# Attention and two expert layers on one core: the order of all five queues worked out by the kernel and fixed by order-only dependences

## The chip, the cores and the metric

One core of one Trainium2 chip runs the whole program. The metric is device time in microseconds (us); lower is better. The five queues are those of TensorE (PE; its weight loads, PEld, are issued by the same queue), VectorE (DVE), ScalarE (ACT), GpSimd (POOL) and SyncE (SP). SP only issues DMAs. Each queue works through its instructions in the order of the program that it was given; an instruction whose inputs are not there holds up all behind it on that queue.

## The reference, cut to what matters

```python
def reference(...):
    # q, k, v: batch 4, heads 8, sequence 1152, width 64
    q_pool = q.reshape(B, H, S // 2, 2, D).mean(axis=3)          # pairs of queries are averaged
    scores = scale * np.matmul(q_pool, k.transpose(0, 1, 3, 2))
    scores = scores - np.max(scores, axis=-1, keepdims=True)
    attn = np.exp(scores)
    attn = attn / (np.sum(attn, axis=-1, keepdims=True) + 1e-09)
    x = np.matmul(attn, v)                                       # then 2304 tokens x 512
    h = x @ w_in                                                 # 512 -> 2048
    x1 = np.maximum(0.01 * h, h) @ w_out                         # 2048 -> 512
    h = np.maximum(np.maximum(x1 @ w1, x1 @ w2), x1 @ w3)        # 512 -> 768, three times
    return h @ w2_out                                            # 768 -> 512
```

The weights of the expert layers come as 64-bit floats.

## The kernel before, in words

The work is cut by batch (4) and, within attention, by pairs of heads (4 a batch, so 16 pairs). A pair goes through two phases: phase 0 has five tiles of 128 queries, phase 1 has four. For each tile `scores` (line 294) multiplies 128 queries with the 1152 keys into three PSUM banks, DVE takes the maximum (`mx`), ACT the exponential with its sum (`p`, `sums`). Queries and keys are split into a high and a low part of fp32r, so a bank takes two matmuls (four for the tile that two heads share). For the first batch (n < NP) the banks are two buffers of two banks, `s_pair`, and one single bank, `s_mid`, with a maximum and an exponential for each (lines 324 to 332); from the second batch on there is one buffer of three banks (lines 334 to 337).

A phase has nine slots, one for each 128 keys. In a slot `probs_t` (line 368) transposes four tiles of `p` on PE into one bank (`pst`), which ACT copies to `pt` (line 377); every third slot of phase 0 `probs_m` adds the shared tile (`psf`, copied by DVE, line 384). One slot after each third, `values` (line 390) multiplies three slots of `pt` with `v` into `pv`: six fp32 matmuls, which the profile shows as twelve. `prep_q` and `prep_k` transpose the queries and keys of the next pair into a bank (`psq`, `psk`), from which ACT writes the high and DVE the low parts (lines 218 to 223 and 254 to 266); SP copies the query parts to the other half of the partitions (line 264).

The banks for `pst`, `psf`, `psq`, `psk`, `psr`, for the expert products (`m`) and for the last layer (`o`) all come from `bank` (line 130): two of them during the first batch, four after it.

`experts` (line 711) runs the expert layers of one batch while the attention of the next batch runs. Each product is up to 12 matmuls of 512 tokens with a chunk of weights (58 chunks a batch). In the first layer its bank goes through ACT (line 731), DVE (732) and POOL (733) before the next product can use it. In the first batch every chunk is loaded as 64-bit numbers, decoded on ACT, DVE and POOL (`decoded` and `split_chunk`, lines 576 to 616) and stored split; in later batches the stored copy is loaded (`load_chunk`, line 631). After the last attention phase the experts of batch 3 run alone, with a second block of the 256 tokens that are left over (`Rest`).

What sets the order: Python emits the work slot by slot, `attention` (line 443) in alternation with `experts`, by the constants of lines 431 to 441. The scheduler of the framework then gives each engine its queue, by the order of emission, by its own costs and by two precedences: `tc.high_priority(offset=EARLY)` with EARLY = 300 for the maxima and exponentials (line 322), and `SOON` = 60 for the evacuation of `pv` (line 419). `on_pe` (line 105) adds order-only dependences: the matmuls of one `values` group stay together, every other PE instruction emitted before the group stays ahead of it, and every one emitted after it stays behind it.

## Time and profile before

| what | value |
|---|---|
| median of 3 runs | 1344.43 us (1343.36 to 1347.69) |
| the profiled execution | 1350.29 us |
| its span, first to last instruction | 1348.5 us |
| PE busy | 1261.8 us, 94% of the span |
| PE weight loads busy | 1016.0 us, 75% |
| DVE, ACT, POOL busy | 637.0 us (47%), 632.5 us (47%), 295.5 us (22%) |
| granted TensorE clock, mean | 0.975 |
| DMA | 193.29 MB, 143 GB/s in the mean |

An engine counts as busy from the start to the end of each of its instructions. Matmuls overlap: a new one starts before the one ahead of it has drained, so the pace of PE is read from starts, not from the mean duration of one. A wait names the instruction that ended it.

### The profile page before, as it was taken

What the parts mean: (1) busy time and instruction counts of PE and PEld (TensorE: products, weight loads), DVE (VectorE), ACT (ScalarE), POOL (GpSimd) and SP (SyncE); (2) the same over time, 40 slices, a digit from 0 to 9 for tenths busy, and PEclk for the clock granted to TensorE, in tenths of its full rate; (3) what the DMA queues carried; (4) which work ended last, traced back from release to release, by engine and by line L of the source; (5) the groups of instructions that cost most, each with busy time, mean ns of one, the idle gap of its engine ahead of it and who ended that gap; (6) DMA issues with size and microseconds to landing.
All of it is one profiled execution on the core that took longest, in us unless ns stands there. A gap on an engine that the chain in (4) does not pass through costs nothing.

```text
span 1348.5 us, 19140 instructions
## 1 busy us (share of the span) xinstructions
PE 1261.8 (94%) x7376; PEld 1016.0 (75%) x7376; DVE 637.0 (47%) x1106; ACT 632.5 (47%) x1253; POOL 295.5 (22%) x265
## 2 busy tenths in 40 slices
PE   5788978899999899999999999999999999999998
PEld 4465646677787778778777878787877788888888
DVE  5755555546566573445456454546464401222110
ACT  5666766656567564444445354535354422112111
POOL 1111023254454330120121010112120002224110
PEclk7888989899999999999999999999999999999999
DMA  5422043566777653354535445545343344333333
GB/s 158 123 75 55 20 133 114 186 228 223 241 239 233 215 178 130 107 155 129 149 129 149 129 142 167 148 128 150 111 144 100 125 152 148 125 125 125 110 125 110
DMA packets 86902, 193.29 MB, mean 143 GB/s; under 512 B 11292, under 2 KB 41756, under 8 KB 86812
## 3 DMA queue, kind: packets, MB, share of 16 engines
q1 hardware_dynamic: 86812, 192.08, 45.7%
q8 instruction: 58, 0.95, 0.3%
q14 instruction: 32, 0.26, 0.1%
HBM read 146.80 MB, written 35.13 MB: 135 GB/s over the span
## 4 chain that ended last, share of the span: by engine, by line
PE 75%; DMA 9%; DVE 8%; ACT 5%; issue 2%; POOL 1%; DVEq 0%; SPq 0%; ACTq 0%; POOLq 0%
PE m L108 39%; PE pv L108 11%; PE s L108 10%; PE pst L108 7%; PE o L108 5%; DMA wraw<-in_moe_w_out_dram 3%; DMA wraw<-in_moe_w_dram 2%; DMA qraw<-in_q_dram 2%; DVE q L259 1%; DMA wraw<-in_moe_w_in_dram 1%; ACT q L255 1%; DVE wmant L596 1%; DVE mx L324 1%; ACT pt L377 1%; DVE mx L334 1%
## 5 line engine op out<-in xcount | busy, mean ns | idle before, releaser
L108 PE MATMUL m<-x,w 128*128 128x512 f32 x1224 | 310.5, 398 | 1.0 <-ACT pt L377 1.0
L108 PEld LDWEIGHTS m<-x,w 128*128 128x128 f32 x1224 | 222.6, 188 | 46.5 <-issue 3.2
L377 ACT COPY pt<-pst 128x512 f32<-128x512 f32 x288 | 167.3, 586 | 183.5 <-PE pst L108 181.9
L334 DVE TENSOR_REDUCE mx<-s 128x1 f32<-128x1152 f32 x108 | 146.3, 1354 | 136.6 <-PE s L108 136.5
L108 PE MATMUL s<-kt,q 128*128 128x384 f32 x840 | 189.2, 359 | 21.1 <-ACT p L335 8.7
L108 PE MATMUL pst<-ident,p 128*128 128x128 f32 x1080 | 174.0, 282 | 10.7 <-ACT pt L377 3.8
L335 ACT ACTIVATE p<-s,mx 128x1152 f32<-128x1152 f32 x108 | 132.2, 1224 | 110.0 <-DVE mx L334 109.4
L108 PEld LDWEIGHTS pst<-ident,p 128*128 128x128 f32 x1080 | 128.1, 142 | 67.2 <-issue 35.4
L108 PEld LDWEIGHTS s<-kt,q 128*128 128x128 f32 x840 | 151.5, 197 | 33.4 <-ACT p L335 10.2
L733 POOL TENSOR_TENSOR g<-t,g 128x512 fp32r<-128x512 f32 x64 | 84.1, 1315 | 355.3 <-DVE g L732 340.8
L108 PE MATMUL m<-g,w 128*128 128x512 f32 x576 | 150.8, 399 | 3.4 <-POOL g L733 3.4
L108 PE MATMUL pv<-pt,v 128*64 128x320 f32 (+1 forms) x1008 | 150.0, 435 | 3.9 <-DVE pt L384 3.6
L108 PEld LDWEIGHTS m<-g,w 128*128 128x128 f32 x576 | 103.4, 188 | 24.3 <-POOL g L733 5.2
L108 PEld LDWEIGHTS pv<-pt,v 128*64 128x64 f32 x1008 | 68.0, 143 | 65.8 <-issue 29.2
L108 PE MATMUL m<-x,wsplit 128*128 128x512 f32 x408 | 107.1, 405 | 4.0 <-ACT t L731 2.4
L612 POOL TENSOR_TENSOR wsplit<-wmant,wsplit 128x512 fp32r<-128x512 f32 x56 | 75.0, 1341 | 100.8 <-ACT wsplit L611 82.2
L731 ACT ACTIVATE t<-m 128x512 f32<-128x512 f32 x80 | 44.2, 554 | 105.4 <-PE m L108 104.7
L108 PEld LDWEIGHTS m<-x,wsplit 128*128 128x128 f32 x408 | 75.2, 191 | 18.6 <-ACT t L731 2.8
L761 DVE TENSOR_TENSOR t<-m,t 128x512 f32<-128x512 f32 (+1 forms) x60 | 38.2, 636 | 78.5 <-PE m L108 71.7
L732 DVE CAST g<-t 128x512 fp32r<-128x512 f32 x64 | 29.2, 458 | 92.5 <-ACT t L731 92.2
L671 POOL TENSOR_TENSOR y<-t,y 128x512 fp32r<-128x512 f32 x24 | 32.2, 1343 | 181.6 <-ACT y L670 181.5
L354 DVE TENSOR_SCALAR p<-p,sums 128x1152 f32<-128x1152 f32 x76 | 69.9, 919 | 2.5
(106 smaller groups left out, 1480.2 us busy)
## 6 DMA issues: line engine op xcount, KB each, us to landing
w<-w SPq DMA_DIRECT2D x168, 512.0 KB
w<-wsplit SPq DMA_DIRECT2D x56, 512.0 KB
wraw<-in_moe_w_out_dram SPq DMA_DIRECT2D x22, 512.0 KB
wraw<-in_moe_w_dram SPq DMA_DIRECT2D x18, 512.0 KB
qraw<-in_q_dram SPq DMA_DIRECT2D x15, 576.0 KB
kraw<-in_k_dram SPq DMA_DIRECT2D x15, 576.0 KB
q<-q SPq DMA_DIRECT2D x52, 160.0 KB
wraw<-in_moe_w_in_dram SPq DMA_DIRECT2D x16, 512.0 KB
```

The source lines that it names most:

```text
L108: mm = f(*args, **kwargs)
L255: nc.scalar.mul(out=hi, in_=src, mul=scale)
L334: nc.vector.tensor_reduce(out=mx[:, 0:1], in_=ps[:, :, 0:SN], axis=AX.XY, op=ALU.max, negate=True)
L335: nc.scalar.activation(out=p[2], in_=ps[:, :, 0:SN], func=ACTF.Exp, bias=mx[:, 0:1], accum_out=rs[:, i:i + 1])
L354: nc.vector.tensor_scalar(out=x, in0=x, scalar1=rs[:, i:i + 1], scalar2=None, op0=ALU.mult)
L377: nc.scalar.copy(out=dst, in_=ps.rearrange("p (j c) -> p j c", j=2))
L612: nc.gpsimd.tensor_tensor(out=t[:, 1], in0=r, in1=t[:, 0], op=ALU.subtract)
L671: nc.gpsimd.tensor_tensor(out=t[:, 1], in0=src, in1=t[:, 0], op=ALU.subtract)
L731: nc.scalar.activation(out=t, in_=ps[:, 0:k.n], func=ACTF.Prelu, alpha=0.01)
L732: nc.vector.tensor_copy(out=gt[:, 0], in_=t)
L733: nc.gpsimd.tensor_tensor(out=gt[:, 1], in0=t, in1=gt[:, 0], op=ALU.subtract)
L761: nc.vector.tensor_tensor(out=t, in0=ps[:, 0:k.n], in1=t, op=ALU.max)
```

## The change

The new kernel emits the same instructions in the same order. The dependences of `on_pe` are gone, so a `values` group is no longer a line that other PE instructions may not cross; instead `on_pe` notes for each PE instruction the unit to which it belongs (three matmuls of a product, one bank of scores, one group of values), and `Pool` notes for each tile the pool and tag from which it came. When all is emitted, `plan()` reads the list of instructions, works out which depends on which, prices each with formulas, and runs a list schedule over the five queues: at each step it takes, of all instructions whose inputs and buffers are there, the one that can start first; of several that can start at the same time, the one emitted first. Tiles of one pool and tag get their buffers in the order of emission, and an instruction that needs a buffer is held back until all tiles emitted before it in that pool and tag have theirs. All transfers share one port of 330 GB/s. The order that comes out is fixed by order-only dependences along each of the five queues. They hold no semaphore. The precedences `EARLY` and `SOON` have no part in the plan. The diff, cut to its core:

```diff
+    slots = {}
+
+    class Pool:
+
+        def __init__(self, name, bufs, stack=ctx, **kwargs):
+            self.name, self.bufs = name, bufs
+            self.pool = stack.enter_context(tc.tile_pool(name=name, bufs=bufs, **kwargs))
+
+        def tile(self, shape, dtype, tag=None, bufs=None, **kwargs):
+            if tag is not None:
+                kwargs["tag"] = tag
+            if bufs is not None:
+                kwargs["bufs"] = bufs
+            t = self.pool.tile(shape, dtype, **kwargs)
+            slots[t.tensor.name] = ((self.name, tag or t.tensor.name), bufs or self.bufs)
+            return t
+
...
-    between = []
-    behind = [None]
-    grouped = [False]
+    units = {}
+    unit = [0]
 
     def on_pe(f, *args, **kwargs):
-
-
         mm = f(*args, **kwargs)
-        if grouped[0]:
-            for other in between:
-                tc.add_manual_dep(mm.ins, other.name, NOSYNC, reason="values of a group stay together")
-            between.clear()
-        if behind[0] is not None:
-            tc.add_manual_dep(mm.ins, behind[0].name, NOSYNC, reason="values of a group stay together")
-        if grouped[0]:
-            behind[0] = mm.ins
-        else:
-            between.append(mm.ins)
+        units[mm.ins.name] = unit[0]
         return mm
 
...
         for c in range(SC):
+            unit[0] += 1
...
-        grouped[0] = True
+        unit[0] += 1
         for g in range(PG):
...
-        grouped[0] = False
+        unit[0] += 1
         marks.append(mm.ins.name)
...
             if x % 3 == 2:
+                unit[0] += 1
                 yield cost(n) * 3
...
                     for x_, (f, a, c) in enumerate(steps):
+                        unit[0] += x_ % 3 == 0
...
+    SEM = 60
+    ENGINES = ("PE", "Activation", "DVE", "Pool", "SP")
+
+    def plan():
+
+        todo = [i for i in nc.cur_bb.bb.instructions if i.opcode not in ("TilePoolBoundary", "RegisterMove")]
+
+        def name_of(engine):
+            return str(engine).split(".")[-1]
+
...
+        nodes = []
+        node_of = {}
+        for i in todo:
+            e = name_of(i.engine)
+            key = units.get(i.name)
+            out = next((n for n, _ in accesses(i.outs)), None)
+            last = nodes[-1] if nodes else None
+            if key is not None and last and last["unit"] == (key, out):
+                last["ins"].append(i)
+            else:
+                nodes.append({"ins": [i], "e": e, "unit": key is not None and (key, out), "out": out})
+            node_of[i.name] = len(nodes) - 1
+        count = len(nodes)
+        before = [set() for _ in nodes]
+        users = {}
+        wrote, read = {}, {}
+        for n, node in enumerate(nodes):
+            for i in node["ins"]:
+                for args, others in ((i.ins, (wrote,)), (i.outs, (wrote, read))):
+                    for t, ap in accesses(args):
+                        users.setdefault(t, set()).add(n)
+                        r = region(ap)
+                        for kind in others:
+                            for m, q in kind.get(t, ()):
+                                if m != n and m not in before[n] and (nodes[m]["e"] == node["e"] or meet(q, r)):
+                                    before[n].add(m)
...
+        for n, node in enumerate(nodes):
+            busy = late = move = 0.0
+            for i in node["ins"]:
+                outs = [ap for _, ap in accesses(i.outs)]
+                cols = size(outs[0].ap) if outs else 512
+                op, e = i.opcode, node["e"]
+                kind = node["out"].rsplit("_", 1)[0] if node["out"] else ""
+                if e == "PE":
+                    if kind == "pv":
+                        one = cols / 1.2
+                    elif kind in ("pst", "psf", "psk", "psr", "psq"):
+                        one = 110.0
+                    else:
+                        one = (cols + 32) / 2.4
+                    busy += one
+                    late = busy + 170
+                elif e == "SP":
+                    busy = 60.0
+                    dst = i.outs[0].bass_ap
+                    move = size([(0, 1)] + [tuple(x) for x in dst.ap]) * 4 / 330.0
+                    late = 3000 + move
+                elif e == "Activation":
+                    late = 185 + 0.8 * cols + 95 * (len(i.outs) > 1) * 2
+                    busy = late - 100
+                elif e == "DVE":
+                    if op == "TensorReduce":
+                        cols = size(next(ap for _, ap in accesses(i.ins)).ap)
+                    psum = any(slots[t][0][0].startswith("ps_") for t, _ in accesses(i.ins))
+                    slow = psum or op == "TensorTensor" or len(list(accesses(i.ins))) > 1
+                    late = 100 + (1.13 if slow else 0.64) * cols
+                    busy = late - 83
+                else:
+                    late = 45 + 2.44 * cols
+                    busy = late - 45
+            if node["out"] and node["out"].startswith("pv"):
+                busy += 320
+                late += 100
+            node["busy"], node["late"], node["move"] = busy, late, move
+
...
+        spent = 0.0
+        prio = []
+        for node in nodes:
+            prio.append(spent)
+            if node["e"] == "PE":
+                spent += node["busy"]
+
...
+        def start_of(n):
+            t = ready[n]
+            for x in need[n]:
+                group = slots[x][0]
+                if queue[group][0] != x or not rooms[group]:
+                    return None
+                t = max(t, rooms[group][0])
+                if group[0] in ("ps_s", "ps_n"):
+                    if narrow[0]:
+                        return None
+                    t = max(t, narrow_at[0])
+            return t
+
+        while done < count:
+            best = None
+            for e in ENGINES:
+                for n in pool[e]:
+                    t = start_of(n)
+                    if t is None:
+                        continue
+                    t = max(t, free[e])
+                    k = (t, prio[n], n)
+                    if best is None or k < best[0]:
+                        best = (k, n, t)
+            assert best is not None, "the plan has no next step"
+            _, n, t = best
+            node = nodes[n]
+            e = node["e"]
+            pool[e].remove(n)
+            order[e].append(n)
+            done += 1
+            free[e] = t + node["busy"]
+            end = t + node["late"]
+            if node["move"]:
+                port = max(port, t + 1500) + node["move"]
+                end = port + 1500
+            for x in need[n]:
+                group = slots[x][0]
+                queue[group].pop(0)
+                heappop(rooms[group])
+            for x in {x for i in node["ins"] for a in (i.ins, i.outs) for x, _ in accesses(a)}:
+                left[x] -= 1
+                until[x] = max(until[x], end + SEM)
+                if not left[x]:
+                    group = slots[x][0]
+                    if group[0] != "dram":
+                        heappush(rooms[group], until[x])
+                    if group[0] == "ps_5":
+                        narrow[0] -= 1
+                        narrow_at[0] = max(narrow_at[0], until[x])
+            for m in after[n]:
+                ready[m] = max(ready[m], end + SEM if nodes[m]["e"] != e else t + node["busy"])
+                waiting[m] -= 1
+                if not waiting[m]:
+                    pool[nodes[m]["e"]].append(m)
+        for e in ENGINES:
+            last = None
+            for n in order[e]:
+                for i in nodes[n]["ins"]:
+                    if last is not None:
+                        tc.add_manual_dep(i, last, NOSYNC, reason="order of the plan")
+                    last = i.name
 
...
         while moe is not None:
             advance()
+        plan()
```

## Rows read from the trace of the kernel before

**Rows 1.** Windows over six stages: length, PE, PEld, DVE, ACT, POOL busy, clock, DMA share, GB/s

```profile
0.00:50.00 50.00, 29.28 (x121) 21.75 (x121) 31.71 (x64) 29.44 (x69) 8.66 (x22) 0.83 0.48 138
50.00:200.00 150.00, 122.60 (x776) 88.27 (x774) 84.39 (x182) 102.61 (x238) 17.48 (x20) 0.92 0.29 75
200.00:300.00 100.00, 86.97 (x473) 66.78 (x472) 52.14 (x75) 59.23 (x111) 39.04 (x32) 0.93 0.56 179
300.00:550.00 250.00, 235.64 (x1361) 188.13 (x1360) 149.14 (x225) 146.62 (x277) 92.54 (x76) 0.97 0.62 202
550.00:1100.00 550.00, 543.18 (x3166) 432.55 (x3164) 274.51 (x479) 252.80 (x470) 85.09 (x64) 1.00 0.44 136
1100.00:1348.50 248.50, 244.08 (x1489) 218.51 (x1488) 45.15 (x81) 41.80 (x89) 52.71 (x52) 1.00 0.40 129
```

**Rows 2.** The same view, 50 to 200 us, PE alone: tile s, then pst, then pv

```profile
50.00:200.00 150.00, 46.32 (x192) 0.92 0.29 75
50.00:200.00 150.00, 36.95 (x241) 0.92 0.29 75
50.00:200.00 150.00, 39.98 (x242) 0.92 0.29 75
```

**Rows 3.** Timeline of PE at full clock: start, us, engine, line, operation, tiles, count

```profile
647.11 0.49 PE L108 MATMUL psf<-ident,p 128*128 128x128 f32 x3
647.44 0.60 PE L108 MATMUL pst<-ident,p 128*128 128x128 f32 x4
...
655.72 0.86 PE L108 MATMUL s<-kt,q 128*128 128x384 f32 x4
656.42 0.85 PE L108 MATMUL m<-g,w 128*128 128x512 f32 x3
```

**Rows 4.** Timeline, 108 to 112 us; in brackets the idle time before, and its releaser

```profile
108.47 0.59 ACT L327 ACTIVATE p<-s,mx 128x384 f32<-128x384 f32 x1
...
109.20 0.62 PE L108 MATMUL s<-kt,q 128*128 128x384 f32 x2 [1.31 <-ACT p L327]
109.75 1.84 PE L108 MATMUL pv<-pt,v 128*64 128x320 f32 x12
...
111.52 0.55 PE L108 MATMUL pst<-ident,p 128*128 128x128 f32 x3
```

**Rows 5.** Timeline, 182 to 187 us

```profile
182.10 1.36 ACT L255 ACTIVATE q<-psq 64x160 fp32r<-64x160 f32 x4
...
185.71 1.09 PE L108 MATMUL psk<-ident,kraw 128*128 128x128 f32 x4 [4.45 <-DVE kt L223]
...
186.73 2.98 PE L108 MATMUL pv<-pt,vx 128*64 128x320 f32 x12
```

**Rows 6.** Timeline, 15 to 19 us

```profile
15.30 1.61 ACT L255 ACTIVATE q<-psq 64x128 fp32r<-64x128 f32 x4 [4.00 <-PE psq L108]
15.64 0.14 DVE L326 TENSOR_REDUCE mx<-mx 128x1 f32<-128x2 f32 x1
...
18.28 0.58 ACT L327 ACTIVATE p<-s,mx 128x384 f32<-128x384 f32 x1
```

**Rows 7.** Waits of PE, 200 to 550 us: total us, times, longest; the two largest

```profile
PE s L108 <- ACT p L335: 8.7, 4, 2.9
PE psk L108 <- ACT acc L743: 3.5, 1, 3.5
```

**Rows 8.** Waits of PE, 550 us to the end, the largest

```profile
PE m L108 <- POOL g L733: 3.4, 4, 1.5
```

**Rows 9.** Groups of instructions by form: count, busy us, mean ns of one, idle before

```profile
L377 ACT COPY pt<-pst 128x512 f32<-128x512 f32 x288 | 167.3, 586 | 183.5 <-PE pst L108 181.9
L334 DVE TENSOR_REDUCE mx<-s 128x1 f32<-128x1152 f32 x108 | 146.3, 1354 | 136.6 <-PE s L108 136.5
L335 ACT ACTIVATE p<-s,mx 128x1152 f32<-128x1152 f32 x108 | 132.2, 1224 | 110.0 <-DVE mx L334 109.4
L354 DVE TENSOR_SCALAR p<-p,sums 128x1152 f32<-128x1152 f32 x76 | 69.9, 919 | 2.5
```

More of the change, by code (lines that the diff above doesn't have):

```diff
@@ L1 @@
 from contextlib import ExitStack
+from heapq import heappop, heappush
 import concourse.bass as bass
@@ L75 @@
-    m_p = ctx.enter_context(tc.tile_pool(name="mb", bufs=1))
-    xf_p = ctx.enter_context(tc.tile_pool(name="xf", bufs=1))
-    pt_p = ctx.enter_context(tc.tile_pool(name="pt", bufs=2))
-    x_p = ctx.enter_context(tc.tile_pool(name="x", bufs=X_BUFS))
-    g_p = ctx.enter_context(tc.tile_pool(name="g", bufs=6))
-    acc_p = ctx.enter_context(tc.tile_pool(name="acc", bufs=1))
-    t_p = ctx.enter_context(tc.tile_pool(name="t", bufs=2))
-    o_p = ctx.enter_context(tc.tile_pool(name="o", bufs=2))
@@ L83 @@
-    w_p = ctx.enter_context(tc.tile_pool(name="w", bufs=W_BUFS))
-    wr_p = ctx.enter_context(tc.tile_pool(name="wr", bufs=2))
-    dram = ctx.enter_context(tc.tile_pool(name="dram", bufs=1, space=bass.MemoryType.DRAM))
-    ps_v = ctx.enter_context(tc.tile_pool(name="ps_v", bufs=1, space=bass.MemoryType.PSUM))
-    ps_m = ctx.enter_context(tc.tile_pool(name="ps_m", bufs=2, space=bass.MemoryType.PSUM))
+    slots = {}
[11 more added lines that the diff above has]
+            return t
@@ new lines @@
+    const = Pool("const", 1)
+    raw_p = Pool("raw", 1)
+    kt_p = Pool("kt", 1)
+    vs_p = Pool("vs", 2)
+    p_p = Pool("p", 9)
+    st_p = Pool("st", 12)
+    rr_p = Pool("rr", 6)
+    m_p = Pool("mb", 1)
+    xf_p = Pool("xf", 1)
+    pt_p = Pool("pt", 2)
+    x_p = Pool("x", X_BUFS)
+    g_p = Pool("g", 6)
+    acc_p = Pool("acc", 1)
+    t_p = Pool("t", 2)
+    o_p = Pool("o", 2)
+    w_p = Pool("w", W_BUFS)
+    wr_p = Pool("wr", 2)
+    dram = Pool("dram", 1, space=bass.MemoryType.DRAM)
@@ L88 @@
+    ps_v = Pool("ps_v", 1, space=bass.MemoryType.PSUM)
+    ps_m = Pool("ps_m", 2, space=bass.MemoryType.PSUM)
     psum = ExitStack()
     ctx.callback(psum.close)
-    ps_5 = psum.enter_context(tc.tile_pool(name="ps_5", bufs=1, space=bass.MemoryType.PSUM))
+    ps_5 = Pool("ps_5", 1, psum, space=bass.MemoryType.PSUM)
     s_pair = [ps_5.tile([128, 2, 512], F32, name=f"s2{i}") for i in range(2)]
@@ L137, in wide_scores @@
             psum.close()
-            ps_s = ctx.enter_context(tc.tile_pool(name="ps_s", bufs=1, space=bass.MemoryType.PSUM))
+            ps_s = Pool("ps_s", 1, space=bass.MemoryType.PSUM)
             ps_w["s"] = ps_s.tile([128, SC, 512], F32, name="s")
-            ps_w["m"] = ctx.enter_context(tc.tile_pool(name="ps_n", bufs=2, space=bass.MemoryType.PSUM))
+            ps_w["m"] = Pool("ps_n", 2, space=bass.MemoryType.PSUM)
         return ps_w["s"]
@@ L582, in decoded @@
         if len(early) < 2:
-            early.append(tc.add_manual_dep(
+            early.append((load.ins.name, marks[GATE]))
+            tc.add_manual_dep(
                 load.ins, marks[GATE],
@@ L586, in decoded @@
                 reason="weights behind the first pair",
-            ))
+            )
         low, high = raw[:, :, 0], raw[:, :, 1]
```

76 lines of the change are left out of this document (69 added, 7 removed).

## The prediction

> **What bounds the kernel now.** I read the windows by stage first [rows 1], because 94% PE busy over the span is a mean over unlike stages. The reader is to see where PE stands idle: 20.7 us of the first 50, 27.4 of the 150 after it, 13.0 of 200 to 300, 14.4 of 300 to 550, then 6.8 in 550 us and 4.4 in the last 248.5. Together that is 86.7 us of 1348.5, and 75.5 of it lies ahead of 550 us. From 550 us on PE is the bound and no order of the queues gives much. Ahead of it, no engine is full: between 50 and 200 us PE is busy 122.6 us, ACT 102.6, DVE 84.4, of 150 [rows 1]. Such a stage is held up by waits, so the order of the queues can matter there.
>
> Second, how much PE time that stage needs. At full clock a transpose starts 0.11 us after the one before (three in 0.33 us) and a score matmul 0.175 us (four in 0.70) [rows 3]; a group of twelve `pv` takes 1.77 us up to the next start [rows 4]. With the counts of 50 to 200 us [rows 2]: 192 scores are 33.6 us, 241 `pst` 26.5, 242 `pv` in groups 35.7, and the other 101 of the 776 PE instructions, small transposes, 11.1 at most. The sum is 107 us, so 43 of the 150 are lost: 27.4 idle, and 16 in a pace below the full one, where the granted clock is 0.92 [rows 1].
>
> Third, the timeline, for what kind of wait it is. At 109.20 us PE has waited 1.31 us for an exponential that frees the single score bank; the `pv` group comes right behind, at 109.75 [rows 4]. At 185.71 PE has waited 4.45 us for a bank: `psk` needs the one that `psq` holds, whose four ACT reads began at 182.10 only, and the DVE reads come after those; the next `pv` group again stands behind it, at 186.73 [rows 5]. In the old code nothing may cross a `pv` group, so the group could not go ahead even if its inputs were there. Early on, a maximum was there at 15.78 us, and its exponential started at 18.28, since ACT had the four reads of the next queries, begun at 15.30, and those of the next keys queued ahead [rows 6].
>
> **The change part by part.** The emitted instructions stay, so PE, ACT, DVE, POOL and DMA work stay; only the places of instructions on the five queues move. The dependences carry no semaphore, so their own cost is nothing in either direction.
>
> *Prices of the plan.* They decide whether the planned order fits the chip. By the diff's formulas a 512-column ACT copy is 595 ns (586 in the trace), a 1152-column maximum 1402 (1354), an exponential 1197 up to the next (1224), a transpose 110, a score matmul 173 (110 and 175) [rows 3, 9]. The one that is far off is the scaling of `p` on DVE, 1402 against 919 ns, 76 times [rows 9]: 37 us of DVE time that is not there. DVE is busy half of 550 to 1100 us [rows 1], so that hides; with its cover gone it would be at most those 37 us. An order made with these prices should fit, save in the first 50 us, where the clock is 0.83 and the plan knows only the full one.
>
> *First 50 us.* The wait of 2.5 us in rows 6 is one of order, and the plan takes the exponential first, as it was emitted first. What is late next is the preparation that it displaces, so I take 3 us of gain. Ends: 8 (three such turns) and a loss of 3 (one such turn the other way, by the wrong clock).
>
> *50 to 200 us.* Idle PE time in which a `pv` group or another ready step stood behind the waiting one can be filled; what then comes late next is ACT, which needs 103 of the 150 us. I take 60% of the 27.4 us idle: 16 us. The ends are 0 (buffers, not order) and 43 (all that is lost); the value lies nearest to the idle time of rows 1, which has waits of both kinds in it.
>
> *200 to 550 us.* 27.4 us idle. The largest wait is for the exponential that frees the one three-bank score buffer, 8.7 us in 4 waits, then 3.5 us for a bank [rows 7]. A step moved forward fills part of it, but the ring of the score buffer itself, six matmuls (1.05), maximum (1.35) and exponential (1.22) [rows 3, 9], does not get shorter. 40%: 11 us. Ends 27 and a loss of 12 (a fourth of the rival below). The loads and stores of decoded weights fall into this stage; the DMA engines are 56 to 62% busy [rows 1], so SP's new order has room.
>
> *550 us to the end.* The largest wait is 3.4 us for the last expert input out of POOL [rows 8]. I take 2 us; ends 7 and a loss of 20, since here PE is full and any wait that the new order adds costs its whole length. In the last 248.5 us only experts run, in the order in which they are emitted: nothing.
>
> Sum: 3 + 16 + 11 + 2 = 32 us. The profiled execution took 1350.3 us, so it would take 1318; the median of the runs is 5.9 us lower, and from it the forecast is 1344.4 − 32 = 1312 us.
>
> **The rivals.** *Slower: softmax loses its precedence.* EARLY puts maxima and exponentials 300 places forward now; the plan puts them in the order of emission, behind whatever ACT or DVE can start first. From the second batch on each of 108 tiles can so be late by one ACT copy (0.586) and one DVE scaling (0.919) [rows 9], 1.5 us, 163 us if all of it ended on PE. It needs 32 us, a fifth, to eat the gain. For it: the score ring is already the largest wait of 200 to 550 us, with precedence [rows 7]. Against it: the 900 us from 200 to 1100 [rows 1] leave 8.3 us to a tile, and its ring takes 3.6. With 30% on PE, 49 us, the time is 1344 + 49 − 32 = 1361.
>
> *Little gain: the gaps are of buffers.* Until 200 us two banks serve all transposes, and `psq` and `psk` hold one until ACT and DVE have read them [rows 5]; the plan hands banks out in the order of emission, so `pst` stays behind `psk` too, and only scores and `pv` can fill. Two `psk` in each of three pairs, each filled by a `pv` group of at most 1.77 us [rows 4], are some 9 us in 50 to 200, and nothing elsewhere: 1335. About half of this case lies within 4 us of no change. That the framework doesn't keep the planned order, or that the plan comes out as the old order, falls in here too.
>
> *Larger gain: the pace comes back with the gaps.* If PE's idle time before 550 us went, the slow pace would go as well: 43 us in 50 to 200, 27 in 200 to 550, 3 and 2 elsewhere: 1269. For it: the clock is 1.00 where PE idles 1%, 0.92 where it idles 18% [rows 1]. Against it: ACT would have to be full for 100 us. The Trainium skill (TensorE: Matmul & The Clock Gate, Part 1: The HAM clock gate) says that "the default state is throttled, and activity releases the throttle", which is the mechanism of this rival and agrees with the clocks of rows 1.
>
> **How the numbers follow.** Forecast, 1283 to 1330: 0.47. Larger gain: 0.10. Little gain: 0.19. Slower: 0.24. A measurement of this kernel tells about 0.3%, 4 us, from no change. Faster by more: 0.47 + 0.10 + half of 0.19 = 0.67; within: 0.09; slower: 0.24. The ends of all terms reach from −85 to +35 us, 1259 to 1379. The range 1268 to 1362 takes in the forecast, the little gain, about half of the larger one and, of the slower case, what lies up to its own value: some 0.83.
>
> **What would show it.** In the new profile PE idle between 50 and 200 us should fall from 27 us to some 11, the clock there rise above 0.92, and the wait of `psk` for DVE disappear or have no `pv` behind it. The last `pv` of the first batch should end some 19 us earlier. From 550 us (shifted by the gain) on, PE should stay 98% busy. The exponential of the first tile should start at about 16 us. The forecast is wrong if waits of `s` for exponentials grow beyond 8.7 us in the second stage or appear behind 550 us (softmax precedence), or if the idle of 50 to 200 us stays above 20 us with `pst` waiting for banks (buffers).

## The result and the profile after

The changed kernel takes 1293.34 us (median, 1291.46 to 1294.59), against 1343.89 (1342.22 to 1347.69) for the kernel before in the same comparison: a ratio of 0.9619, 95% interval 0.9595 to 0.9643, so 51 us or 3.8% faster.

Its profiled execution took 1292.83 us, of which the span is 1291.0. The first view is that of the cores: span and mean granted clock.

```profile
core 0: 1291.0 us, clock 0.989
```

The span is 57.5 us shorter than that of before. The medians differ by 51, because the profiled execution of before lay 5.9 us above its median and this one 0.5 us below. The working below adds up to 57.5; some 6 of it belong to that execution and can't be placed.

Next the page's line of the engines, then the windows by stage of the kernel after; the columns are those of [rows 1], with other stages.

```profile
PE 1236.5 (96%) x7376; PEld 1004.0 (78%) x7376; DVE 634.8 (49%) x1106; ACT 635.3 (49%) x1253; POOL 294.5 (23%) x265
```

```profile
0.00:50.00 50.00, 27.67 (x119) 23.62 (x120) 32.10 (x69) 29.26 (x71) 8.65 (x22) 0.80 0.49 137
50.00:200.00 150.00, 135.31 (x905) 98.98 (x905) 93.45 (x192) 115.77 (x263) 27.22 (x28) 0.98 0.36 101
200.00:300.00 100.00, 98.70 (x561) 77.59 (x560) 65.34 (x103) 72.07 (x137) 45.10 (x38) 1.00 0.69 222
300.00:550.00 250.00, 242.82 (x1442) 194.43 (x1443) 151.33 (x234) 150.22 (x279) 86.93 (x72) 1.00 0.64 201
550.00:1100.00 550.00, 544.92 (x3213) 441.27 (x3211) 255.13 (x445) 238.67 (x445) 88.00 (x69) 1.00 0.44 138
1100.00:1291.00 191.00, 187.02 (x1144) 168.11 (x1142) 37.46 (x66) 29.32 (x62) 38.55 (x39) 1.00 0.37 121
```

Read first the PE column against the length of the stage. Idle is now 22.3, 14.7, 1.3, 7.2, 5.1 and 4.0 us; before it was 20.7, 27.4, 13.0, 14.4, 6.8 and 4.4 [rows 1]. Over the span that is 54.5 against 86.7, 32 us less. Then the busy time itself: 1236.5 against 1261.8 us for the same 7376 matmuls, 25 us less. So of the 57.5 us, 32 are gaps that were filled, and 25 are matmuls that ran at a better pace. The clock column belongs to the second: 0.98 and 1.00 where it was 0.92 and 0.93 to 0.97 [rows 1].

Windows at fixed times hold other work once the work has moved. To place the gain I take marks that both kernels pass. They come from the view of one tile; the last numbers ahead of the semicolon are the first and the last start. The marks are the first and last `values` group of the first batch (`vx` is its last block), the first product with a reloaded chunk of weights (`m<-x,w`), and the last product of the last layer (`o`). Before:

```profile
L108 PE MATMUL pv<-pt,v x1008: 379/432/796, 47.5 to 1102.5; 128*64 128x320 f32 x84, 128*64 128x256 f32 x84
...
L108 PE MATMUL pv<-pt,vx x72: 379/433/796, 175.4 to 220.0; 128*64 128x320 f32 x36, 128*64 128x256 f32 x36
...
L108 PE MATMUL m<-x,w x1224: 387/390/677, 543.7 to 1313.8; 128*128 128x512 f32 x175
...
L108 PE MATMUL o<-w,y x432: 277/283/385, 799.5 to 1339.9; 128*128 128x256 f32 x144
```

After:

```profile
L123 PE MATMUL pv<-pt,v x1008: 379/432/484, 50.4 to 1044.3; 128*64 128x320 f32 x84, 128*64 128x256 f32 x84
...
L123 PE MATMUL pv<-pt,vx x72: 379/431/639, 159.9 to 189.6; 128*64 128x320 f32 x36, 128*64 128x256 f32 x36
...
L123 PE MATMUL m<-x,w x1224: 387/390/499, 487.4 to 1256.2; 128*128 128x512 f32 x175
...
L123 PE MATMUL o<-w,y x432: 277/283/387, 743.6 to 1282.4; 128*128 128x256 f32 x144
```

| stretch | before | after | difference | predicted |
|---|---|---|---|---|
| start to the first `pv` | 47.5 | 50.4 | +2.9 | −3 |
| to the last `pv` of the first batch | 172.5 | 139.2 | −33.3 | −16 |
| to the first product with a reloaded chunk | 323.7 | 297.8 | −25.9 | −11 |
| to the last `o` | 796.2 | 795.0 | −1.2 | −2 |

So the gain sits in the two stages in which it was expected, at twice the expected size; the start went the other way, and the full stage behind gave nothing. In the two stretches PE's idle time fell by 18.1 us (from 31.7 to 13.6) and 14.4 (from 23.1 to 8.7); the other 15.2 and 11.5 us are less busy time.

What the new order looks like is seen where [rows 5] showed the old one, at the preparation of a pair (timeline after: start and length in us, then engine, line, operation, tiles, count):

```profile
164.91 0.27 PE L123 MATMUL psq<-ident,kraw 128*64 128x128 f32 x1
...
165.90 1.40 ACT L261 ACTIVATE q<-psq 64x160 fp32r<-64x160 f32 x4
166.13 1.83 PE L123 MATMUL pv<-pt,vx 128*64 128x320 f32 x12
...
168.12 0.66 PE L123 MATMUL psk<-ident,kraw 128*128 128x128 f32 x4
```

The same four ACT reads of `psq` hold the bank. The `pv` group that used to stand behind `psk` now goes ahead of it, at 166.13, and PE works while the bank is read.

The waits of PE between 50 and 200 us (us in total, times, longest) have become small; the largest, and the one of [rows 5]:

```profile
PE pst L123 <- DVE kt L229: 2.9, 3, 1.2
...
PE psk L123 <- DVE kt L229: 1.3, 2, 1.1
```

Between 200 and 550 us the largest is 2.3 us, and the wait of `s` for exponentials, 8.7 us before [rows 7], is not in the list.

### The profile page after: what moved, and what is told of

It is laid out like the page before. It is cut to its first block, busy times and chain, and to the rows that moved or that the text cites. A ratio compares the mean times of both kernels' runs of the same rounds, so it can differ in the third digit from the quotient of the medians.

```text
span 1291.0 us, 19125 instructions
## 1 busy us (share of the span) xinstructions
PE 1236.5 (96%) x7376; PEld 1004.0 (78%) x7376; DVE 634.8 (49%) x1106; ACT 635.3 (49%) x1253; POOL 294.5 (23%) x265
## 5 line engine op out<-in xcount | busy, mean ns | idle before, releaser
L123 PE MATMUL m<-x,w 128*128 128x512 f32 x1224 | 303.9, 395 | 0.4 <-PE psk L123 0.4
L123 PE MATMUL s<-kt,q 128*128 128x384 f32 x840 | 188.5, 361 | 17.1 <-DVE kt L229 10.2
L123 PE MATMUL pst<-ident,p 128*128 128x128 f32 x1080 | 170.5, 279 | 14.3 <-DVE kt L229 8.9
L123 PEld LDWEIGHTS s<-kt,q 128*128 128x128 f32 x840 | 146.3, 196 | 23.4 <-DVE kt L229 10.9
L123 PE MATMUL m<-g,w 128*128 128x512 f32 x576 | 145.3, 396 | 0.0
L123 PE MATMUL pv<-pt,v 128*64 128x320 f32 (+1 forms) x1008 | 140.8, 414 | 0.0
L123 PEld LDWEIGHTS pv<-pt,v 128*64 128x64 f32 x1008 | 64.9, 136 | 59.4 <-issue 24.9
L361 DVE TENSOR_SCALAR p<-p,sums 128x1152 f32<-128x1152 f32 x76 | 67.3, 885 | 2.7
```

The costliest lines, as they stand in the source:

```text
L123: mm = f(*args, **kwargs)
L361: nc.vector.tensor_scalar(out=x, in0=x, scalar1=rs[:, i:i + 1], scalar2=None, op0=ALU.mult)
```

## The experiments

Two theories stood at the outset. The first is that of the prediction: work that is ready may cross a `values` group, so PE's gaps are filled. The rival is that the prices and the joint order make the gain: every queue is laid out with knowledge of the others, and it matters little what may cross what. A third question was the forecast's slower case, the precedence of the softmax. All kernels do the whole computation. Differences below are of medians against the kernel before in the same comparison; the change itself gave −50.6 us.

### One queue alone, or all but one

Only PE's order is fixed; ACT, DVE, POOL and SP are left to the framework:

```diff
-        for e in ENGINES:
+        for e in ("PE",):
```

> The plan is made as in the changed kernel, but only the PE queue is fixed; ACT, DVE, POOL and SP get their order from the framework's scheduler, with its EARLY and SOON precedences. Theory (the gain is of PE's queue, where ready steps no longer stand behind a waiting one): most of the 51 us stays, 1295 to 1312 us. Rival (the gain is of the order on ACT and DVE, which free the banks sooner): less than a third stays, 1327 us or more.

Measured: 1338.71 us, ratio 0.9939 (0.9913 to 0.9964), −7 us. Most of the gain is gone, as under the rival; that the rival's cause, the order of ACT and DVE, doesn't bring it either, the next two runs show. The marks show where PE's order alone helps. It takes the first batch, from the first to the last `pv`, in 145.0 us (172.5 before, 139.2 with the whole plan). It loses most of that again elsewhere: 55.9 us to the first `pv`, where before took 47.5, and 806.4 in the last stretch, where before took 796.2.

The other way round, the four other queues are fixed and PE is free:

```diff
-        for e in ENGINES:
+        for e in ENGINES[1:]:
```

> The reverse: ACT, DVE, POOL and SP are fixed by the plan, PE gets its order from the framework's scheduler, without any dependence that holds the groups of values together. Theory (PE's queue): most of the gain is gone, 1325 us or more. Rival (ACT's and DVE's queues): 1310 us or less.

Measured: 1347.05 us, 1.0010 (0.9994 to 1.0027), no gain. But this run has a price of its own. With PE left to the framework and no line around `pv`, the matmuls of a group come apart. Timeline of PE in this kernel:

```profile
106.12 0.65 PE L123 MATMUL pv<-pt,v 128*64 128x256 f32 x4
106.70 0.55 PE L123 MATMUL pst<-ident,p 128*128 128x128 f32 x3
...
107.29 0.65 PE L123 MATMUL pv<-pt,v 128*64 128x256 f32 x4
```

and the page's line of the engines:

```profile
PE 1283.7 (95%) x7376; PEld 1003.8 (75%) x7376; DVE 630.2 (47%) x1106; ACT 624.9 (46%) x1253; POOL 295.0 (22%) x265
```

The `pv` matmuls run in 189 stretches instead of 95. Four of 256 columns take 0.58 us up to the next start, where twelve in a row take 1.45. PE idles 24 us less than before, but is busy 22 us more, at a mean clock of 0.990. One gain and one loss of the same size: so a second run had to take the tearing out.

It fixes the same four queues, with a plan that knows the old line around `pv`, and PE runs in the framework's order under that line:

```diff
+        if grouped[0]:
+            for other in between:
+                tc.add_manual_dep(mm.ins, other.name, NOSYNC, reason="values of a group stay together")
...
-        for e in ENGINES:
+        for e in ENGINES[1:]:
```

> The plan of e3_plan_with_line, but only ACT, DVE, POOL and SP are fixed by it; PE gets its order from the framework's scheduler under the old dependences of the PE helper, so the groups of values stay whole. In e2_all_but_pe PE's order was free and 189 runs of pv stood where 95 had been, so it could not tell a bad fit of the queues from torn groups; this one can. Theory (the gain comes from queues that were laid out together; a part of them alone gives little): 1333 to 1348 us, like before. Rival (the order of ACT and DVE does carry a gain and torn groups ate it): 1328 us or less, near the 1322 of e3_plan_with_line.

Measured: 1347.75 us, 1.0025 (1.0011 to 1.0038), 3 us slower. Between 50 and 200 us it is the kernel before again: PE is busy 123.9 us at a clock of 0.91, against 122.6 and 0.92 [rows 1].

What follows: PE alone gives 7 of 51 us, the other four alone nothing. The two parts don't add up to the whole: that neither brings the gain without the other is shown. The reading of it is argued: an order planned for one queue supposes what the others do at that time, and where they do something else, the queue stands at instructions whose inputs are late. Of the four others, SP can be left out:

```diff
-        for e in ENGINES:
+        for e in ENGINES[:4]:
```

> The whole plan, but SP's queue, the order in which DMAs are issued, is left to the framework's scheduler. If the gain of 200 to 550 us hangs on the order of the weight loads and stores, 1305 us or more, with the loss behind the end of the first batch's attention. If PE, ACT, DVE and POOL carry it, 1289 to 1299 us.

Measured: 1295.83 us, 0.9626 (0.9606 to 0.9645): the same as the whole change, within the intervals.

### The line around the values group

The plan keeps the old rule that nothing on PE crosses a `pv` group; all five queues are fixed:

```diff
+        group, others = None, []
+        for n, node in enumerate(nodes):
+            if node["e"] != "PE":
+                continue
+            if group is not None:
+                before[n].add(group)
+            if node["out"].startswith("pv"):
+                before[n].update(others)
+                group, others = n, []
+            else:
+                others.append(n)
```

> The whole plan on all five queues, but with the old rule in it: every PE instruction emitted before a group of values stays ahead of it and every one emitted after it behind it. Theory (it is the line at each group of values that held ready steps back): PE idle of 50 to 200 us goes back above 20 us, and the time to 1318 us or more. Rival (better prices and orders everywhere, the line costs little): 1300 us or less.

Measured: 1321.75 us, 0.9817 (0.9789 to 0.9845), −24 us. Its window of 50 to 200 us:

```profile
50.00:200.00 150.00, 126.83 (x817) 90.49 (x814) 87.38 (x185) 105.97 (x245) 19.35 (x22) 0.90 0.31 82
```

and its three largest waits of PE there, all for a transpose's bank to be read:

```profile
PE psq L123 <- ACT pt L384: 6.7, 2, 3.4
PE psk L123 <- DVE kt L229: 3.6, 3, 2.1
PE psk L123 <- DVE kspare L229: 2.9, 2, 2.0
```

PE idles 23 us there, 27 before and 15 after. So with the line kept the first batch gains little, and the waits of [rows 5] stay.

The opposite, the kernel before with the line taken out and no plan:

```diff
-        if grouped[0]:
-            for other in between:
-                tc.add_manual_dep(mm.ins, other.name, NOSYNC, reason="values of a group stay together")
...
-        if grouped[0]:
-            behind[0] = mm.ins
-        else:
-            between.append(mm.ins)
         return mm
```

> The kernel before, with the order-only dependences of its PE helper taken out and no plan: the framework's scheduler alone sets all queues, and the six matmuls of a group of values may be torn apart. If taking the line away is all that it needs, 1310 us or less. If the order must also be planned with durations near the chip's, 1330 us or more; torn groups of values can make it slower than the 1344 of before.

Measured: 1332.40 us, 0.9894 (0.9863 to 0.9925), −14 us, with the `pv` matmuls in 159 stretches.

What follows: freedom to cross the group is worth about 27 us of the 51 (0.9817 against 0.9619), and the order that the plan finds within the old rule is worth the other 24. Both theories hold, each for about half, and the marks give each its own place. With the line kept the first batch takes 164.0 us, 25 more than in the change, but the stretch behind it 299.8, 2 more than in the change and 24 less than before. So the line held up the first batch; behind it the gain comes without crossing it. Freedom without a plan gives 14, with torn groups; the change keeps them whole by planning each as a unit.

### The precedence of the softmax

In the plan, order of emission settles ties. Here maxima and exponentials are ranked as if emitted 20 us of PE work sooner:

```diff
+        for n, node in enumerate(nodes):
+            if node['out'] and (node['out'].startswith('mx') or any(o.opcode=='Activation' and len(o.outs)>1 for o in node['ins'])):
+                prio[n] -= 20000.000000
```

> The whole plan of the changed kernel, but where several instructions can start at the same time, maxima and exponentials count as emitted 20 us of PE work earlier, about what EARLY gave them before. If the lost precedence of softmax costs time (the slower rival of the prediction), 1287 us or less. If it does not, 1290 us or more; much above 1300 would say that precedence takes ACT and DVE from what frees the banks.

Measured: 1309.03 us, 0.9733 (0.9707 to 0.9759): 15 us slower than the change. So such a precedence costs in the plan, and the forecast's slower case had the wrong sign. The loss lies ahead of the last `pv` of the first batch: 55.4 us to the first `pv` and 148.1 from there, against 50.4 and 139.2 in the change. The two stretches behind, where the forecast feared for 108 tiles, take 299.4 and 795.3 us, against 297.8 and 795.0. The next run does the reverse: the same lines, 10 us behind.

```diff
-                prio[n] -= 20000.000000
+                prio[n] -= -10000.000000
```

> The whole plan, but where several instructions can start at the same time, maxima and exponentials count as emitted 10 us of PE work later than they are. e7_precedence moved them earlier and took 16 us. If what e7_precedence lost is that the reads that free the transpose banks waited behind softmax, the reverse costs nothing or gains a little, 1284 to 1296 us, and the waits of PE for banks read by DVE in the first batch shrink. If softmax is on the path itself, 1300 us or more.

Measured: 1285.11 us, 0.9556 (0.9529 to 0.9582), the lowest of all kernels here and ahead of the change, whose interval begins above it, at 0.9595. The marks show where. The first `pv` comes at 44.5 us in place of 50.4:

```profile
L123 PE MATMUL pv<-pt,v x1008: 379/432/484, 44.5 to 1034.7; 128*64 128x320 f32 x84, 128*64 128x256 f32 x84
```

The stretches behind it are 138.4, 294.8 and 795.1 us, against 139.2, 297.8 and 795.0 in the change. So 6 of the 9.6 us of span are won in the start, where the preparation of keys and queries goes ahead of the softmax of the tile that is there. PE's waits of `s` for the low part of the keys (`kt`), all in the first 50 us, show it; in the change, then in this kernel:

```profile
PE s L123 <- DVE kt L229: 10.2, 2, 6.1
...
PE s L123 <- DVE kt L229: 4.1, 1, 4.1
```

The time is as expected, the reason is not: PE's waits for transpose banks read by DVE didn't shrink (up to 200 us they are 8.7 us in sum, against 8.3 in the change). What comes sooner is the keys.

### The prices

The next run takes the prices for what an instruction streams alone: no semaphore time, no fixed part on any engine, no latency of a transfer.

```diff
-    SEM = 60
+    SEM = 0
...
-                    late = 3000 + move
+                    late = move
...
-                    late = 185 + 0.8 * cols + 95 * (len(i.outs) > 1) * 2
-                    busy = late - 100
+                    late = busy = 0.8 * cols
...
-                    late = 45 + 2.44 * cols
-                    busy = late - 45
+                    late = busy = 2.44 * cols
...
```

> The whole plan of the changed kernel with other prices: columns over a rate alone on PE, ACT, DVE and POOL, no fixed part, no drain, no 320 ns for a group of values, no latency of semaphores and DMAs. Theory (an order fits the chip only as far as its prices do): half of the gain or more goes, 1315 us or more. Rival (any list schedule in the order of emission without the line does it): 1300 us or less.

Measured: 1322.74 us, 0.9819 (0.9785 to 0.9854): 28 of the 51 us are lost. Two more runs ask which price it is. The first keeps the fixed parts of the engines' busy times and drops what comes behind them: semaphore, drain, and a transfer's latency.

```diff
-    SEM = 60
+    SEM = 0
...
-                    late = 3000 + move
+                    late = move
...
-            node["busy"], node["late"], node["move"] = busy, late, move
+            node["busy"], node["late"], node["move"] = busy, min(late, busy) if not move else late, move
...
-                port = max(port, t + 1500) + node["move"]
-                end = port + 1500
+                port = max(port, t) + node["move"]
+                end = port
```

> The whole plan with the engines' times as they are, but no latencies: no drain, no 60 ns for a semaphore, results there when the engine is free, DMAs at their port time alone. It splits e6_bare_prices (1323 us, fixed parts and latencies both gone). If the latencies are what makes the order fit, most of those 29 us come back as loss, 1313 us or more. If it is the fixed parts of the engines' times, 1303 us or less.

Measured: 1362.71 us, 1.0121 (1.0089 to 1.0152), 18 us slower than before. The second drops the latency of transfers alone:

```diff
-                    late = 3000 + move
+                    late = move
...
-                port = max(port, t + 1500) + node["move"]
-                end = port + 1500
+                port = max(port, t) + node["move"]
+                end = port
```

> The whole plan with drains and semaphores as they are, and only the fixed 3 us of a DMA taken out of it. It splits e11_no_latency (1363 us). If it is the DMA's latency that the order has to know, because weights are thought to be there too early and PE stands before them, 1320 us or more. If it is the drains and semaphores between the engines, 1291 to 1303 us.

Measured: 1346.24 us, 0.9990 (0.9969 to 1.0011). The whole gain of this plan is gone with one price. Much of where it went is seen on ACT, which decodes the loaded weights. Its waits for these loads between 200 and 550 us (us in total, times, longest), before:

```profile
ACT wraw L590 <- DMA wraw<-in_moe_w_out_dram: 24.9, 13, 4.4
...
ACT wraw L590 <- DMA wraw<-in_moe_w_dram: 23.9, 15, 3.1
...
ACT wraw L590 <- DMA wraw<-in_moe_w_in_dram: 11.6, 9, 3.0
```

after:

```profile
ACT wraw L598 <- DMA wraw<-in_moe_w_dram: 7.8, 9, 1.4
...
ACT wraw L598 <- DMA wraw<-in_moe_w_out_dram: 5.8, 5, 2.2
...
ACT wraw L598 <- DMA wraw<-in_moe_w_in_dram: 2.8, 2, 1.5
```

with no latency of transfers in the plan:

```profile
ACT wraw L598 <- DMA wraw<-in_moe_w_out_dram: 36.0, 16, 4.4
...
ACT wraw L598 <- DMA wraw<-in_moe_w_dram: 31.9, 16, 3.4
...
ACT wraw L598 <- DMA wraw<-in_moe_w_in_dram: 15.2, 8, 3.5
```

That is 60.4, 16.4 and 83.1 us. ACT is only half busy, so that its standing there costs PE is not plain from the sums; one place in the timeline of the last kernel shows how:

```profile
435.96 1.34 DVE L341 TENSOR_REDUCE mx<-s 128x1 f32<-128x1152 f32 x1
...
439.63 0.68 ACT L598 ACTIVATE wraw<-wraw 128x512 f32<-128x512 f32 x1 [2.93 <-DMA wraw<-in_moe_w_dram]
...
440.19 1.22 ACT L342 ACTIVATE p<-s,mx 128x1152 f32<-128x1152 f32 x1
...
441.56 1.86 PE L123 MATMUL s<-kt,q 128*128 128x384 f32 x7 [3.45 <-ACT p L342]
```

The maximum is there at 437.30. ACT stands at the read of a load until 439.63, and the plan, which knew no latency, had taken the load to be there sooner; the exponential comes behind it at 440.19, and `s`, whose bank it frees, at 441.56, after PE has waited 3.45 us. The row of PE names the exponential; the cause is the load, at whose read ACT stood before it came to the exponential. In this kernel such waits of `s` are 14.3 us in 9 between 200 and 550 us, and the stretch from the last `pv` of the first batch to the first reloaded chunk takes 333.1 us against 297.8. That the gain of this plan hangs on this price is shown. That all of the loss goes this way is not: of the 55 us by which the two spans differ, 35 lie in that stretch, 8 in the first batch and 12 behind.

What the transfers took in the kernel after (KB each, median us from issue to landing):

```profile
w<-w SPq DMA_DIRECT2D x168, 512.0 KB, 4.2
...
wraw<-in_moe_w_out_dram SPq DMA_DIRECT2D x22, 512.0 KB, 10.0
wraw<-in_moe_w_dram SPq DMA_DIRECT2D x18, 512.0 KB, 8.2
...
wraw<-in_moe_w_in_dram SPq DMA_DIRECT2D x16, 512.0 KB, 5.0
```

In the plan a load of 512 KB that finds the port free lands after 4.6 us, 3 and 1.6 for the bytes; one that finds it taken waits for it there too. The first and the last row are near 4.6, the other two take about twice that. How much of their time is waiting at the port, which the plan counts, the rows don't tell, and that a longer price would gain more was not tried. The Trainium skill (DMA: Bandwidth & Descriptors, Anatomy of one DMA) gives, for transfers issued by POOL, a fixed 2.0 us and the bytes over 436 GB/s, an estimate of 3.2 us here; in this trace, where SP issues them and other transfers run, they take more.

One thing stays open: the bare prices, which lack the latency too, keep 22 us of gain and the two runs with better prices elsewhere keep none. ACT's waits for loads are smaller with the bare prices (48.3 us between 200 and 550) than in the other two (71.1 without any latency, 83.1 without that of transfers); why the orders come out so differently was not tried. Over all plans of the five queues, or of four without SP, these waits and the stretch behind the first batch go together: with 13 to 17 us of waits in the span (the change, the plan with the line, both ranks of the softmax, without SP, the slow start below) the stretch takes 295 to 300 us, with 48 (bare prices) 309, with 75 and 95 (the other two) 341 and 333. Few such waits are not enough, though: where only the four other queues are fixed they are 12 us (PE free) and 17 us (under the line), and the stretch takes 322 and 317.

### A slow start in the plan

The last run adds three edits to the best one: PE's busy time doubled in the plan for the first 35 us, the price of the scaling of `p` mended, and in the first batch the scores of the next phase emitted two slots later.

```diff
-    EARLIER = 5
+    EARLIER = 3
...
-                    slow = psum or op == "TensorTensor" or len(list(accesses(i.ins))) > 1
+                    wide = sum(size(ap.ap) > 1 for _, ap in accesses(i.ins))
+                    slow = psum or op == "TensorTensor" or wide > 1
...
-            free[e] = t + node["busy"]
-            end = t + node["late"]
+            cold = node["busy"] if e == "PE" and t < 35000 else 0.0
+            free[e] = t + node["busy"] + cold
+            end = t + node["late"] + cold
...
-                ready[m] = max(ready[m], end + SEM if nodes[m]["e"] != e else t + node["busy"])
+                ready[m] = max(ready[m], end + SEM if nodes[m]["e"] != e else free[e])
```

> A version meant to beat the changed kernel: softmax later as in e10_softmax_later, the DVE scaling of p priced near its 0.9 us instead of 1.4, PE priced at half speed for the first 35 us, and the scores of the first batch emitted two slots later (EARLIER 3 for 5). If the 50 us up to the first group of values were a matter of order and prices, it comes earlier by 3 us or more and the time is 1280 to 1288 us. If that stretch is a chain of loads, splits and maxima, no change there, 1288 to 1297 us.

Measured: 1290.61 us, 0.9583 (0.9559 to 0.9607), 5 us behind the kernel that it starts from in the median, though the intervals overlap, with the first `pv` at 47.2 us in place of 44.5. Each forecast is half met: the first `pv` comes 3 us earlier than in the change, but the time is not below 1288. The three edits together don't help; which of them costs was not tried.

## Why the prediction was right, and where it was off

The direction and the place held, and so did the mechanism in the first batch: ready work stood behind a `values` group, and it no longer does. Behind the first batch PE's waits were filled too, but not by crossing that line. The time came out 19 us below the forecast of 1312 and inside the range; its main term was too small. By its steps:

*What bounds the kernel.* Right. The gain lies ahead of 550 us, and from there to the last `o` the two kernels differ by 1.2 us.

*The sum of 32 us.* It was made from PE's idle time alone, and PE's idle time fell by 32.2 us. By stage the terms were off both ways: −1.6 (said 3), 12.7 (said 16), 18.9 (said 11) and 2.2 (said 2) of idle in the windows of [rows 1] and of after.

*The term left out.* 25 us of the gain are pace: less busy time for the same matmuls. The prediction had worked out 16 us of slow pace in 50 to 200 us from [rows 1 to 4], and then put its return into a rival with a chance of 0.10, as if the pace came back only where the gaps went altogether. It came back with a part of them. From the clocks, (1 − 0.975) × 1348.5 = 34 us of full clock were missing before and (1 − 0.989) × 1291 = 14 after, so 20 of the 25 us are of that kind, by an estimate that takes the clock's mean over the whole span. This is the step that was mis-sized: a gap filled in a stage whose clock is below 1.00 should have been counted with its share of the pace, 16 us beside the 27 of idle time in 50 to 200. The 16 is itself somewhat low, since the prediction priced each `pv` group at the 1.77 us of 320 columns, and one of 256 takes 1.45.

How firmly clock and idle time hang together was not isolated. At single places the windows show one behind the other (columns as in [rows 1]). Before, at the wait of [rows 5] and behind it:

```profile
180.00:185.00 5.00, 1.02 (x9) 0.79 (x9) 2.34 (x10) 4.51 (x13) 1.06 (x2) 1.00 0.08 19
185.00:190.00 5.00, 4.29 (x19) 2.31 (x20) 4.17 (x6) 1.42 (x3) 1.84 (x2) 0.66 0.75 206
```

After, at the emptiest 5 us that are left between 50 and 200:

```profile
170.00:175.00 5.00, 2.71 (x20) 1.69 (x18) 4.29 (x10) 3.32 (x8) 0.57 (x1) 1.00 0.84 253
175.00:180.00 5.00, 4.97 (x24) 3.47 (x24) 2.82 (x4) 3.07 (x6) 0.70 (x1) 0.66 1.02 255
```

In such windows the clock falls below 0.9 at five places of that stage before and at two after, each time behind a window with a gap. But not every gap has a fall behind it, and by stage the two don't go in step. Between 50 and 200 us the runs show idle 27, 26, 23, 18 us at clocks of 0.92, 0.91, 0.90, 0.94 (before, the four queues under the line, the plan with the line, PE alone), but 18, 16, 15, 14 us at 0.99, 0.98, 0.98, 0.99 (no latency of transfers, bare prices, the change, all but PE). The kernel with precedence has 18.5 us at 0.91, and in the first 50 us it has a clock of 0.93 with PE busy 26.5 us, where the change has 0.80 with 27.7. So the sum of idle time alone doesn't set the clock. That the filled gaps brought the pace back is seen at places like these; that it is so for all 20 us remains argued. The rule of the Trainium skill that the prediction cited (TensorE: Matmul & The Clock Gate, Part 1) agrees with the falls behind gaps; that a low clock is the default these traces don't show, for in the first 10 us PE is busy 1.8 us and the granted clock is 1.00, in both kernels.

*First 50 us.* Wrong in sign, by 6 us. What [rows 6] promised did come. The same place in the timeline after:

```profile
15.00 0.16 DVE L333 TENSOR_REDUCE mx<-mx 128x1 f32<-128x2 f32 x1
15.20 0.80 ACT L261 ACTIVATE q<-psq 64x128 fp32r<-64x128 f32 x2 [3.79 <-PE psq L123]
15.80 0.55 ACT L334 ACTIVATE p<-s,mx 128x384 f32<-128x384 f32 x1
...
17.32 0.80 ACT L261 ACTIVATE q<-psq 64x128 fp32r<-64x128 f32 x2
```

The exponential starts at 15.80, as said. But the reads of `psq` are cut in two by it, and the preparation that the prediction named as next in line is late. PE waits 10.2 us for the low part of the keys in the change, in the row shown above; before, it was less:

```profile
PE s L108 <- DVE kt L223: 4.1, 1, 4.1
```

An early exponential is worth nothing here while the keys are missing. The run with the softmax placed later, whose exponential starts at 18.62, near the 18.28 of before, is back at 4.1 us of this wait and wins 6 us.

*50 to 200 us.* All waits of `psk` for ACT and DVE in this stage fell from 9.5 to 2.9 us (of these DVE's `kt` from 5.5 to 1.3), and the `pv` group went ahead of `psk`; idle came to 14.7 us (said 11) and the clock to 0.98 (said above 0.92). The stretch up to the last `pv` of the first batch is 33 us shorter, where 16 were said, and that `pv` starts 30 us earlier, where 19 were said. Of the 33 us, 18 are idle time and 15 are pace, which is the excess.

*200 to 550 us.* 26 us against 11, of which 14 are idle time and 11.5 pace. The step took the waits of `s` for exponentials as the ring of the score buffer, which no order shortens, and gave 40% of the idle time back. PE now has other work while the ring goes round, so the waits went and 70% of the idle time came back. What gave it that work is not the freedom to cross a `values` group, since with the line kept the stretch is nearly as short (299.8 us against 297.8). And the step didn't look at ACT's own waits: 60.4 us at loads of weights, which the plan cut to 16.4. It named the loads as SP's matter, where there is room, and not as something at which ACT stands.

*Prices.* The forecast compared the engines' prices with the trace, found them good, and passed over the price of a transfer; with that alone taken out the plan gains nothing. It also set the 595 ns after which the plan takes a copy's result to be there against the 586 for which the copy keeps ACT busy; for the next start on ACT the plan counts 495, and what that costs was not tried. The scaling of `p`, the one price that it found wrong, was mended only together with two other edits, in a kernel that is no faster, so its own cost stays open.

*The slower rival.* It fell, with the opposite sign: precedence costs 15 us, and ranking the softmax later gains 8. The delay of up to 1.5 us a tile didn't come. Over the 108 tiles, read from the timelines, the maximum starts 0.54 us behind its scores before and 0.14 after in the mean, and the exponential 0.24 us behind its maximum before and 0.18 after. Without precedence, ACT and DVE are free for the softmax sooner than with it in the old order.

*The rival of little gain.* In the plan that keeps the line, 24 us are won, so gaps of banks are not all there is; but its reading of what can fill the wait of `psk` fits the timeline, where it is a `pv` group.

## What to carry to other kernels

Where several in-order queues feed each other, plan them together: here PE's queue alone gave 7 us, the four others alone none, four of the five (without SP) 49 and all five 51. Price what the planned instruction waits for, a transfer's landing above all; with that price alone left out the plan gained nothing. A queue that is half busy can still hold up the bound engine, if it stands at a load with an exponential behind it. When gaps in a stage with a clock below 1.00 are to be filled, give the pace that may come back a term of its own: here it was nearly as large as the gaps, though no run isolated it.

## What the runs showed of the hardware

- A group of twelve fp32 `pv` matmuls that is cut into fours costs PE time: three times 0.58 us against 1.45 for 256 columns, three times 0.69 against 1.77 for 320, so 0.15 us for each cut, in the run with PE free. With 189 stretches instead of 95 that is 14 of the 22 us by which PE was busier there, at a mean clock of 0.990, so a high clock and little idle time alone don't make a fast kernel.
- Loads of 512 KB by one queue landed in 4.2 us in the median when they brought stored weights (issued from 467 us on, mostly in stages in which the DMA engines are 0.37 to 0.44 busy), and in 5.0, 8.2 and 10.0 us, by source, when they brought the 64-bit ones. Those with 8.2 were all issued between 317 and 405 us, in a stage in which the DMA engines are 0.64 busy.
